# Round 0 of an RWKV6 and MLP kernel: taken whole, in place of its first 128 steps going ahead

## The chip, the cores and the metric

The kernel runs on one core of a Trainium2 chip. Its engines are TensorE (PE, with its weight loads shown apart as PEld), VectorE (DVE), ScalarE (ACT), GpSimd (POOL) and SyncE (SP, which here only starts transfers). The metric is device time in microseconds (us), lower is better. A time is the median of some runs; a profile is one execution of its own.

## The reference

An attention block without softmax (a decaying state, step by step) over 4 batches, 8 heads, 768 steps and 48 dimensions of a head, and then a layer norm and an MLP with a residual, all in float32.

```python
for t in range(S):
    kt, vt, rt, wt = (k[:, :, t], v[:, :, t], r[:, :, t], w[:, :, t])
    cur = np.einsum('bhd,bhe->bhde', u[None] * kt, vt)
    y[:, :, t] = np.einsum('bhd,bhde->bhe', rt, state + cur)
    state = wt[:, :, :, None] * state + np.einsum('bhd,bhe->bhde', kt, vt)
...
xn = (x - mu) / np.sqrt(var + 1e-06) * g_ln
ch = np.maximum(xn @ w_ch1, 0.0) @ w_ch2
return (x + ch).astype(np.float32)
```

Here `x` is `y` with the 8 heads side by side (384 columns), `w_ch1` is 384 x 1536 and `w_ch2` 1536 x 384.

## The kernel before

**Tiles and rounds.** The work is cut into 8 rounds: a batch and a half of its steps (384 steps, three tiles of 128) for all 8 heads. A round has two units of four heads, each with two pairs of heads. In a chunk of 64 steps the recurrence is written as products: squares of steps against steps, built up over six levels (`quads` on PE, `grow` on DVE, `keep` on DVE), and a state passed between chunks (`states`).

**A round in order.** Natural tiles of w, k and r are loaded (`load`, tile `nat`), turned by PE through an identity (`turn`, tiles `w_ps`, `k_ps`, `r_ps`) and copied from the accumulation banks by ACT (or DVE in round 0). `totals` multiplies the decays up level by level (`tot`, `decay`; DVE or POOL). At every level PE multiplies squares (tile `a`), DVE scales k and r by the decay (`grow`) and copies the squares that this level gives into `A`, by a mask (`keep`). ACT copies the last level. k is turned back (`turn_k`, `kn_ps`), then PE makes the chunks' states, DVE scans them (`s`, `last`), ACT exchanges halves (`rx`, `sx`), PE makes the outputs, and DVE adds the step's own term (`own`, `own_term`, tiles `rk`, `vo`) and writes `x`. `normalize` and `turn_x` give `xf`. The MLP has a first product (`h_ps` to `h`, 12 blocks) and a second one (`o`).

**The MLP's weights** come in as 24 blocks of 384 KB (`convert`, tile `raw`, four buffers). Each is put into another form by three ACT and two DVE instructions: 12 blocks of w_ch1 (`w`, `held`) and 12 of w_ch2 (`ffn`, `rest`). From round 1 on the first product runs in three cheaper products of split operands, for which w_ch1 is split by `halve` (`wh`, `wl`).

**What sets the order.** The order of all instructions is written by a planner (`Plan.order`) as the program is built. It goes through the operations with costs and priorities written beside them, gives each to an engine when its operands, its buffer and its engine are free by these costs, takes the one with the lowest priority number first, and so fixes the order of each engine's queue. An operation with `port=True` also keeps DVE and POOL from running port operations side by side in the plan. The queues run in order on the chip; SP's queue holds all loads but some of round 0's, which ACT starts. Where the plan leaves PE without work for over 0.4 us before its 90th us, it puts in products of nothing (`idle`). There are two pairs of accumulation banks for the tile `a` and four banks for the others.

**Round 0 in two parts.** `parts_of_round` gives round 0 two parts, the first 128 steps of all heads and the other 256, and every other round one. `front`, `normalize`, `turn_x` and `first_product` are called once for each part, and the first part has a round's lead in priority (`urgent`). Its loads (`load_first`) take all 8 heads at once, one for each of w, k and r, into tiles held for them from the start. The shifts and joins of the first six weight blocks have priority -6. The masks of the levels (`build_mask`) are built by POOL with priority `lev - 40` and `port=False`.

Of the kernel before, what the change touches and what calls it, by code (L numbers as in the profile page):

```python
# [9 lines left out]
F32 = mybir.dt.float32  # L10
# [6 lines left out]
ALU = mybir.AluOpType  # L17
# [243 lines left out]
def kernel(  # L261
# [57 lines left out]
    def tile_(tag, name, shape, dtype=F32):  # L319
        if name in tiles:  # L320
            return tiles[name]
        if tag == "a":
            tiles[name] = a_homes[plan.place[name]]
            return tiles[name]
        if tag == "nat" and name.startswith("nat_"):
            tiles[name] = nat_homes[plan.place[name]]
            return tiles[name]
        if tag == "b":
            t = banks.tile([P, 512], dtype, tag=f"b{plan.place[name]}", name=name)
            tiles[name] = t[:, 0 : shape[1]]  # L330
            return tiles[name]
        t = homes.tile(shape, dtype, tag=f"{tag}{plan.place[name]}", name=name)
        tiles[name] = t
        return t
# [11 lines left out]
    plan.hold("vo", "nat_r_0")  # L346
    tile_("vo", "nat_r_0", [P, NH * ROW])
    for name in ("nat_r_1", "nat_k_1", "nat_w_1", "nat_k_0", "nat_w_0"):
        plan.hold("nat", name)
        tile_("nat", name, None)  # L350
# [27 lines left out]
    for nm in "wkr":  # L378
        POOL.memset(tiles[f"nat_{nm}_0"][:, 0 : HP - D], 0.0)
    for nm in "wk":  # L380
        POOL.memset(tiles[f"nat_{nm}_0"][:, NH * ROW :], 0.0)
# [33 lines left out]

    SRC = {"w": w, "k": k, "r": r}
    NA = U * NP

    def parts_of_round(rnd):
        return [(rnd, 0, TT)] if rnd else [(0, 0, 1), (0, 1, TT - 1)]

    def urgent(part, stage):
        rnd, c0, nc = part
        return at(rnd - (nc == 1), stage)

    def cost(part, fixed, whole):
        return fixed + (whole - fixed) * part[2] / TT

    def of(part, t, per):

        _, c0, nc = part
        return t.rearrange("p (a x) -> p a x", a=NA)[:, :, c0 * per : (c0 + nc) * per]

    def keys_of(nm, part, us=both_units):
        rnd, c0, _ = part
        return [(f"{nm}{rnd}", NP * uu + pr, c0) for uu in us for pr in pairs]

    def groups_of(part):  # L440

        n = min(NP if part[0] == 0 else 1, NA) if part[2] > 1 else NA
        return [(a, n) for a in range(0, NA, n)]

    GAP = HP - D

    def natural(nm, part, a):

        rnd, c0, _ = part
        if rnd == 0:  # L450
            return f"nat_{nm}_{c0}", a
        return f"nat_{nm}{U * rnd + a // NP}", a % NP

    def row_of(part):

        return part[2] * D, (GAP if part[2] == 1 else 0)

    def load_first(nm, part, eng, pri):
        _, c0, nc = part
        b, f = rounds[0]  # L460
        name = natural(nm, part, 0)[0]
        queue = SP if eng == "SP" else ACT
        row, margin = row_of(part)

        def go():
            queue.dma_start(
                out=tiles[name][:, margin : margin + H * row].rearrange("p (h x) -> p h x", h=H),
                in_=SRC[nm][b, :, ds(f * RN + c0 * P, nc * P)]
                .rearrange("h (p c) d -> p h (c d)", p=P),
            )  # L470

        plan.add(eng, 0.5, go, w=[name], r=[], pri=pri, lat=2.0, size=0.8 + 0.3 * (nc > 1))

    def load(nm, q):
        b, f, g = units[q]
        name = f"nat_{nm}{q}"

        def go():
            to = tile_("nat", name, None)
            if q // U < ROWS:  # L480
                SP.dma_start(
                    out=to[:, 0 : NH * ROW].rearrange("p (h x) -> p h x", h=NH),
                    in_=SRC[nm][b, ts(g, NH), ds(f * RN, RN)]
                    .rearrange("h (p c) d -> p h (c d)", p=P),
                )
                return
            for c in range(TT):
                SP.dma_start(
# [4 lines left out]
        cost_, size = (0.5, 0.8) if q // U < ROWS else (1.65, 1.2)  # L493
        plan.add(
            "SP", cost_, go, w=[name], new=[("nat", name)], pri=at(q // U, "wrk".index(nm)), lat=2.0,
            size=size,
        )
# [4 lines left out]
    def turn(nm, part, a0, na, stage):  # L502
        rnd, c0, nc = part
        name, ps = f"{nm}{rnd}", f"{nm}_ps{rnd}_{c0}_{a0}"
        rows = rnd < ROWS
        row, margin = row_of(part)

        def go():
            t = tile_("b", ps, [P, na * nc * P])
            for a in range(na):  # L510
                key, pr = natural(nm, part, a0 + a)
                for c in range(nc):
                    to = ts(a * nc + c, P)
                    if not rows:
                        both = by_tile(tiles[key])[:, c, ts(pr, 2)].rearrange("p j d -> p (j d)")
                        PE.transpose(t[0:PD, to], both[:, 0:PD], ident)
                        continue


                    at_ = 2 * pr * row + c * D + margin  # L520
                    second, first = ds(at_ + row - HP, PD), ds(at_, HP)
                    PE.transpose(t[0:PD, to], tiles[key][:, second], ident)
                    PE.transpose(t[0:HP, to], tiles[key][:, first], ident)

        def keep(e="ACT"):
            to = of(part, tile_(nm, name, [P, U, W])[0:PD].rearrange("p u t -> p (u t)"), P)
            to, ps_ = to[:, a0 : a0 + na], tiles[ps][0:PD].rearrange("p (a x) -> p a x", a=na)
            if rows and nc > 1:
                to = to.rearrange("p a (s c) -> p a s c", c=nc)
                ps_ = ps_.rearrange("p a (c s) -> p a s c", c=nc)  # L530
            (DVE.tensor_copy if e == "DVE" else ACT.copy)(out=to, in_=ps_)

        n = na * nc
        keys = [(name, a0 + a, c0) for a in range(na)]
        new = [(nm, name)] if a0 == c0 == 0 else []
        plan.add(
            "PE", 0.11 * n * (1 + rows), go, count=2 * n * (1 + rows),
            r=[natural(nm, part, a0)[0]] + keys, w=[ps], new=[("b", ps)] + new,
            pri=urgent(part, stage), lat=0.17,
        )  # L540
        copy = 0.1 + 0.12 * n
        plan.add(
            ("ACT", "DVE") if rnd == 0 else "ACT", (copy, copy + 0.05) if rnd == 0 else copy, keep,
            r=[ps], w=keys, pri=urgent(part, stage) + EVICT / 2,
        )

    def totals(part):
        rnd, c0, nc = part
        tot, dec = f"tot{rnd}", f"decay{rnd}"
        costs = list(zip((1.0, 0.55, 0.4, 0.3, 0.25, 0.2), (1.5, 0.9, 0.58, 0.42, 0.34, 0.25)))  # L550
        for lev in range(NLEV):
            def go(e, lev=lev):
                if lev == 0:
                    tile_("tot", tot, [P, U * W])
                    tile_("decay", dec, [P, U * NM])
                pair = level_total(part, lev).rearrange("p a (q two) -> p a q two", two=2)
                BY[e].tensor_tensor(
                    out=level_total(part, lev + 1), in0=pair[..., 0], in1=pair[..., 1], op=ALU.mult
                )
            plan.add(  # L560
                EITHER, [cost(part, 0.17, x) for x in costs[lev]], go,
                r=keys_of("w", part) if lev == 0 else [(tot, lev, c0)],
                w=[(tot, lev + 1, c0)] if lev < NLEV - 1 else [(dec, c0)],
                new=[("tot", tot), ("decay", dec)] if lev == c0 == 0 else [],
                pri=urgent(part, 6 + lev),
            )

    def level_total(part, lev):
        rnd = part[0]
        if lev == 0:  # L570
            t = tiles[f"w{rnd}"].rearrange("p u t -> p (u t)")[0:PD]
        elif lev == NLEV:
            t = tiles[f"decay{rnd}"][0:PD]
        else:
            n = U * W >> lev
            t = tiles[f"tot{rnd}"][0:PD, U * W - 2 * n : U * W - n]
        return of(part, t, P >> lev)

    def own(part, us):
        rnd, c0, nc = part  # L580
        heads, h0 = NH * len(us), NH * us[0]
        kk, kr = (natural(nm, part, NP * us[0])[0] for nm in "kr")
        rk, o, row = f"rk{rnd}_{c0}_{us[0]}", f"own{rnd}", f"own_row{rnd}"
        rows = rnd < ROWS
        by_row = rows and nc > 1
        row_, margin = row_of(part)
        margin += (rnd == 0) * h0 * row_

        def parts():

            t = tile_("rk", rk, [P, NH * ROW])[:, 0 : nc * heads * D]
            if rows:
                views = [
                    t_.rearrange("p (h c d) -> p c h d", h=heads, c=nc) for t_ in (
                        tiles[kk][:, margin : margin + heads * row_],
                        tiles[kr][:, margin : margin + heads * row_], t,
                    )
# [4 lines left out]
            return views + [u_bc[:, None, ds(h0, heads)].broadcast_to([P, nc, heads, D])]  # L602
# [9 lines left out]
        def third():  # L612
            if by_row:
                t = tile_("own_row", row, [P, TT, H])[:, 0:nc]
            else:
                t = tile_("own", o, [P, TT, H])[:, c0 : c0 + nc]
# [1061 lines left out]
```

## Time and profile before

| | us |
|---|---|
| median of 3 runs | 537.83 |
| lowest and highest | 537.31, 539.05 |
| the profiled execution, whole | 537.31 |
| its span in the profile | 535.4 |

How to read the profile: one execution is recorded instruction by instruction, in us from the span's start. Busy time is the time in which an engine has at least one instruction under way; consecutive instructions overlap a little, so a row's start-to-start distance is shorter than its duration. All operations are recorded by one helper (line 49), so groups are told apart by tile names: `k<-k,tot` reads `k` and `tot` and writes `k`. `x6` is the number of instructions in a merged row; a float32 product takes two. PE's groups by busy time:

| group | instructions | busy us |
|---|---|---|
| second product of rounds 0 to 4, `o<-ffn,h` | 360 | 124.7 |
| squares, states and outputs, `a`, weight loads 63.1 | 4608 (squares) | 69.4 |
| first product of round 0, 128x128 | 72 | 9.4 |
| first product of round 0, 128x256 | 72 | 18.3 |
| `idle` | 34 | 13.1 |

The last row adds its three shapes (9.0, 3.0 and 1.1). POOL's ten mask selections, eight mask copies and two `mask_and` lie between 1.85 and 11.1 us.

### The profile page before, as it was taken

Reading aid. Unit: us, or ns where it says so; the run is one execution under the profiler, and the core shown is the slowest. Engines: PE = TensorE matmul, PEld = TensorE weight load, DVE = VectorE, ACT = ScalarE, POOL = GpSimd, SP = SyncE. Lnnn points to the kernel's source line nnn. Section 1 sums busy time; section 2 is a strip of 40 time slices with the busy share of each in tenths; the row PEclk is TensorE's granted clock in tenths of the full one; section 3 lists DMA queues with packets and bytes.
Section 4 is the critical chain, followed back from the end, with each engine's and each line's share of the span. In section 5 each row is a group of like instructions: output and inputs, shape, how many; then the busy total and the mean of one; then the engine's idle time right before and its main releaser. Section 6 shows DMA issues by size and latency. Waiting matters only on the chain.

```text
span 535.4 us, 20629 instructions
## 1 busy us (share of the span) xinstructions
PE 521.3 (97%) x8994; PEld 434.4 (81%) x8994; DVE 403.2 (75%) x845; ACT 269.0 (50%) x602; POOL 73.0 (14%) x106
## 2 busy tenths in 40 slices
PE   8999899999999999999999999999999999999995
PEld 6778788776989676889766998669867999999994
DVE  6898969797999988999765787546555856656554
ACT  3798868962395532663630885046721434332321
POOL 6212201531203041112110000002200000000000
PEclk9999989999999999999999999999999999999999
DMA  9874864378525646576111415014101322213101
GB/s 222 248 209 142 192 175 105 72 185 237 158 49 105 157 85 131 113 148 146 61 30 37 112 39 139 2 40 115 46 15 60 104 60 88 89 45 108 56 0 45
DMA packets 122362, 55.84 MB, mean 104 GB/s; under 512 B 93984, under 2 KB 119200, under 8 KB 122272
## 3 DMA queue, kind: packets, MB, share of 16 engines
q1 hardware_dynamic: 119152, 53.54, 39.3%
q10 hardware_dynamic: 3120, 0.98, 1.0%
q8 instruction: 71, 1.16, 0.9%
q14 instruction: 19, 0.16, 0.1%
HBM read 45.05 MB, written 7.10 MB: 97 GB/s over the span
## 4 chain that ended last, share of the span: by engine, by line
PE 85%; DVE 7%; DMA 2%; issue 1%; POOL 1%; SPq 1%; ACT 1%; DVEq 0%; POOLq 0%; ACTq 0%
PE a L49 24%; PE o L49 21%; PE h_ps L49 18%; PE hd_ps L49 7%; PE w_ps L49 3%; PE k_ps L49 2%; PE r_ps L49 2%; PE o_2P L49 2%; PE kn_ps L49 2%; DVE x L49 2%; PE xT_ps L49 2%; PE idle L49 1%; DVE k L49 1%; PE o_2D L49 1%; DVE r L49 1%
## 5 line engine op out<-in xcount | busy, mean ns | idle before, releaser
L49 PE MATMUL o<-ffn,h 128*128 128x384 f32 x360 | 124.7, 491 | 0.0
L49 PEld LDWEIGHTS o<-ffn,h 128*128 128x128 f32 x360 | 65.4, 190 | 37.6
L49 PEld LDWEIGHTS a<-r,k 48*60 48x60 f32 (+5 forms) x4608 | 63.1, 126 | 19.6 <-issue 8.5
L49 ACT COPY h<-hd_ps 128x384 f32<-128x384 f32 x84 | 39.9, 479 | 71.6 <-PE hd_ps L49 69.8
L49 DVE SCALAR_TENSOR_TENSOR h<-h_ps,h 128x384 f32<-128x384 f32 x84 | 46.5, 555 | 34.7 <-PE h_ps L49 34.2
L49 PE MATMUL a<-r,k 48*60 48x32 f32 (+5 forms) x4608 | 69.4, 212 | 2.0 <-DVE r L49 1.3
L49 DVE TENSOR_TENSOR k<-k,tot 112x768 f32<-112x768 f32 (+1 forms) x50 | 41.4, 828 | 29.0 <-PE a L49 18.6
L49 PE MATMUL h_ps<-xhl,wl 128*128 128x384 f32 x252 | 60.8, 349 | 0.3
L49 PE MATMUL h_ps<-xhl,wh 128*128 128x384 f32 x252 | 57.9, 338 | 0.0
L49 PE MATMUL hd_ps<-xd,d 128*128 128x384 f32 x252 | 55.4, 347 | 0.0
L49 PEld LDWEIGHTS h_ps<-xhl,wl 128*128 128x128 f32 x252 | 43.7, 188 | 3.5 <-ACT h L49 1.1
L49 PEld LDWEIGHTS h_ps<-xhl,wh 128*128 128x128 f32 x252 | 45.3, 188 | 0.0
L49 PEld LDWEIGHTS hd_ps<-xd,d 128*128 128x128 f32 x252 | 43.9, 188 | 1.1
L49 DVE COPY_PREDICATED A<-mask,a 128x768 f32<-128x768 int8 (+2 forms) x36 | 39.3, 1092 | 0.9 <-PE a L49 0.9
L49 DVE TENSOR_TENSOR r<-r,tot 112x768 f32<-112x768 f32 (+1 forms) x50 | 39.6, 791 | 0.0
L49 ACT ACTIVATE hH<-h 128x384 fp32r<-128x384 f32 x36 | 18.8, 526 | 41.0 <-DVE h L49 41.0
L49 ACT ACTIVATE h<-h 128x384 f32<-128x384 f32 x48 | 25.1, 526 | 20.3 <-DVE h L49 20.1
L49 POOL TENSOR_TENSOR vo<-v,own 128x576 f32<-128x576 f32 (+1 forms) x12 | 13.5, 1121 | 141.3 <-DVE x L49 107.3
L49 ACT COPY w<-w_ps 112x384 f32<-112x384 f32 (+1 forms) x31 | 14.3, 489 | 34.3 <-PE w_ps L49 34.0
L49 DVE SCALAR_TENSOR_TENSOR hL<-h,hH 128x384 fp32r<-128x384 f32 x36 | 20.0, 555 | 14.3 <-ACT hH L49 14.0
L49 ACT COPY A<-a 32x384 f32<-32x384 f32 (+2 forms) x36 | 15.6, 433 | 27.8 <-PE a L49 27.5
L49 PE MATMUL h_ps<-xf,w 128*128 128x128 f32 (+1 forms) x144 | 27.7, 343 | 0.1
(120 smaller groups left out, 1020.3 us busy)
## 6 DMA issues: line engine op xcount, KB each, us to landing
d<-w1d SPq DMA_DIRECT2D x84, 192.0 KB, 2.7
raw<-in_moe_w_ch_dram SPq DMA_DIRECT2D x24, 384.0 KB, 4.3
v<-in_v_dram SPq DMA_DIRECT2D x48, 96.0 KB, 2.8
out_dram<-x SPq DMA_DIRECT2D x24, 192.0 KB, 1.9
nat<-in_w_dram SPq DMA_DIRECT2D x36, 96.0 KB, 3.5
nat<-in_k_dram SPq DMA_DIRECT2D x36, 96.0 KB, 3.2
nat<-in_r_dram SPq DMA_DIRECT2D x36, 96.0 KB, 3.0
w1d<-w1diff SPq DMA_DIRECT2D x12, 192.0 KB, 2.7
```

The lines of the kernel that those rows point to most:

```text
L49: ins = self.tc.keep_in_program_order(f(*args, **kw))
```

## The change

Round 0 becomes one part like the other rounds. `front`, `turn`, `totals`, `own`, `quads`, `grow`, `keep`, `keep_last`, `exchange_r`, `turn_k`, `load_v`, `own_term`, `states`, `outputs`, `normalize` and `turn_x` lose the part and work on a round or on a unit; `first_product` goes back into `mlp`. Round 0's six loads are one for each of w, k, r and each unit, of 384 steps and four heads, from SP for one unit and ACT for the other. Only the two r tiles have homes held from the start, and five fills on POOL (128x192) take the place of three of 128x16 and two of 128x192. The masks' priority is `lev` and no longer `lev - 40`, still with `port=False`; the shifts and joins of the first six weight blocks have the priority of the others; `g` is loaded with priority 20 and no longer -10. Tiles in the four banks have the shape asked for and no longer a whole bank, and the squares lie in the first 384 columns of a bank. The planner and its costs for the other rounds stay.

```diff
-    plan.hold("vo", "nat_r_0")
-    tile_("vo", "nat_r_0", [P, NH * ROW])
-    for name in ("nat_r_1", "nat_k_1", "nat_w_1", "nat_k_0", "nat_w_0"):
-        plan.hold("nat", name)
-        tile_("nat", name, None)
+    for q in both_units:
+        plan.hold("vo", f"nat_r{q}")
+        tile_("vo", f"nat_r{q}", [P, NH * ROW])
...
-    for nm in "wkr":
-        POOL.memset(tiles[f"nat_{nm}_0"][:, 0 : HP - D], 0.0)
-    for nm in "wk":
-        POOL.memset(tiles[f"nat_{nm}_0"][:, NH * ROW :], 0.0)
+    for t in nat_homes:
+        POOL.memset(t[:, NH * ROW :], 0.0)
...
-    def parts_of_round(rnd):
-        return [(rnd, 0, TT)] if rnd else [(0, 0, 1), (0, 1, TT - 1)]
-
-    def urgent(part, stage):
-        rnd, c0, nc = part
-        return at(rnd - (nc == 1), stage)
...
-        first = -6 if i < FC // 2 else pri
...
-        plan.add("DVE", 0.32, shift, w=[key], pri=first, port=True)
-        plan.add("DVE", 0.56, join, r=[rest_], w=[key], pri=first, port=True)
+        plan.add("DVE", 0.32, shift, w=[key], pri=pri, port=True)
+        plan.add("DVE", 0.56, join, r=[rest_], w=[key], pri=pri, port=True)
...
-    def first_product(part):
-        rnd, c0, nc = part
-        steps = slice(c0 * P, (c0 + nc) * P)
-        for f in range(FC):
...
+                def go(f=f, ps=ps, g=g, cols=cols):
+                    t = tile_("b", ps, [P, RN])
+                    for kc in range(KC):
+                        PE.matmul(
+                            t, tiles[f"w1_{g}"][:, kc, cols], tiles[f"xf{rnd}_{kc}"],
+                            start=kc == 0, stop=kc == KC - 1,
+                        )
...
-    def front(part):
-        rnd, c0, nc = part
+    def front(rnd):
...
             for i, nm in enumerate("wkr"):
-                load_first(nm, part, ("SP", "ACT")[(i + c0) % 2], at(c0 - 1, i))
-        if rnd == c0 == 0:
+                for q, eng in zip(qs, ("SP", "ACT")):
+                    load(nm, q, eng, i)
+        if rnd == 0:
...
-                plan.add(
-                    "POOL", 1.7, lambda lev=lev: build_mask(lev), r=["wide"], w=[("mask", lev)],
-                    pri=lev - 40, port=False,
-                )
+                plan.add("POOL", 1.7, lambda lev=lev: build_mask(lev), r=["wide"], port=False, w=[("mask", lev)], pri=lev)
...
-        w=["g"], pri=-10, lat=2.0, size=0.2,
+        w=["g"], pri=20, lat=2.0, size=0.2,
...
-    for part in parts_of_round(0):
-        front(part)
-        norm(part)
-        if part[1] == 0:
-            for i in range(len(parts)):
-                convert(i)
-        first_product(part)
-    mlp(0)
+    front(0)
+    for i in range(len(parts)):
+        convert(i)
+    back(0)
```

## Prediction

> **What bounds the kernel now.** I read the page's busy shares and chain first, then busy time by stretches, the chain in order of time, and the timeline where the change acts.
>
> ```profile
> PE 521.3 (97%) x8994; PEld 434.4 (81%) x8994; DVE 403.2 (75%) x845; ACT 269.0 (50%) x602; POOL 73.0 (14%) x106
> ...
> PEclk9999989999999999999999999999999999999999
> ...
> PE 85%; DVE 7%; DMA 2%; issue 1%; POOL 1%; SPq 1%; ACT 1%; DVEq 0%; POOLq 0%; ACTq 0%
> ```
>
> TensorE (PE) sets the time. What can change it is only PE's own work, and the time in which PE has none: its gaps and its filler products (tile `idle`). The stretches say where those are:
>
> ```profile
> 15.00:65.00 50.00, 48.42 (x1178) 40.00 (x1171) 45.46 (x126) 44.26 (x110) 10.43 (x14) 1.00 0.71 191
> 61.30:69.30 8.00, 5.13 (x114) 4.12 (x115) 7.86 (x11) 4.85 (x11) 1.43 (x1) 0.97 0.80 189
> 69.30:77.60 8.30, 8.30 (x129) 7.00 (x128) 3.80 (x6) 6.24 (x15) 0.00 (x0) 0.83 0.82 212
> 77.60:96.10 18.50, 18.50 (x458) 16.23 (x456) 17.02 (x26) 16.58 (x39) 4.27 (x3) 1.00 0.37 93
> 96.10:535.40 439.30, 431.13 (x7084) 359.19 (x7083) 322.43 (x663) 194.88 (x429) 48.77 (x52) 1.00 0.35 88
> ```
>
> Columns: stretch, length, busy PE, weight loads, VectorE (DVE), ScalarE (ACT), GpSimd (POOL), granted clock, DMA share, GB/s. From 77.6 us PE is saturated, with 8.2 us open in the last 439.3. So the change is decided before about 96 us, where round 0's second product starts. In 15 to 65 DVE (91%) and ACT (88.5%) are both nearly full. The chain, then the timeline:
>
> ```profile
> 28.96 2.58 PE idle L49 x8
> ...
> 62.63 4.93 DMA nat<-in_k_dram
> ...
> 76.45 1.30 PE h_ps L49 x6
> ...
> 93.44 1.15 PE kn_ps L49 x12
> ...
> 96.11 2.13 PE o L49 x6
> ```
>
> ```profile
> 35.33 0.42 DVE L49 TENSOR_TENSOR r<-r,tot 112x256 f32<-112x256 f32 x1
> 35.67 0.42 DVE L49 TENSOR_TENSOR k<-k,tot 112x256 f32<-112x256 f32 x1
> 61.49 0.95 DVE L49 TENSOR_TENSOR k<-k,w 112x768 f32<-112x768 f32 x1
> 62.36 0.95 DVE L49 TENSOR_TENSOR r<-r,w 112x768 f32<-112x768 f32 x1
> ```
>
> ```profile
> 60.57 0.59 SPq L49 DMA_DIRECT2D raw<-in_moe_w_ch_dram  x1
> 61.34 1.25 SPq L49 DMA_DIRECT2D vx<-v  x2
> 62.63 1.80 SPq L49 DMA_DIRECT2D nat<-in_k_dram  x3
> ```
>
> Until about 33 us PE is filled up with `idle`: it waits for the first 128 steps to pass through attention. At 62.6 it waits for a load of k that SP could issue only after a weight load (`raw`), whose buffer ACT had to free.
>
> **PE's lost time before.** I count PE's own work by rows and subtract it. 72 turning instructions a round at 0.13 (x6 in 0.80): 9.4. The six levels' squares (x96): 1.58, 1.56, 1.45, 1.37, 1.21, 0.95: 8.1. Turning k back 1.15, states 1.3, outputs 2.9, xT 1.1. Round 0 without its first product: 24.0. First product: 12 x 0.72 (36 instructions in 4.29) for 128 steps and 12 x 1.30 for 256. At 61.3 us PE has done 24.0 + 8.6 + round 1's turning 9.4 and level 0 1.6 = 43.6, so 17.7 us are lost. At 77.6 it has 55.0 (four more blocks 5.2, levels 1 and 2 3.0, 24 turnings of round 2 3.2), so 22.6 are lost: 4.9 between, 1.4 of them in the 0.83 clock of 8.3 us.
>
> **The change, part by part.**
>
> *The masks.* Their instructions stand in the same place on POOL in both programs, ahead of all tensor work; only the fills before them differ (five of 128x192 at 0.26 for three of 0.11 and two of 0.26: +0.45 us). Before, the last mask lands at 11.1 us; after, the first level that needs one copies from about 21. Cost nothing, covered by 9 us. So the masks move nothing; what moves is round 0.
>
> *First product whole.* 36 products of 128x384 (1.94 for x6, as the rows of `o`) for 36 of 128 and 36 of 256: 12 x (0.72 + 1.30 - 1.94) = 1.0 us of PE saved.
>
> *When it can start (T).* Four parts:
> (a) Six loads of 288 KB go first (SP w, k, r; ACT the same for the other unit), then u, four weight blocks and six v, each issue past the eighth waiting for the landing of an older one. DMA moved 214, 210, 242, 320 GB/s in the four slices of 2 to 10 us, 1.97 MB, against 1.77 MB needed: the last r lands near 9. PE starts turning at about 4.4 as now, 12 groups x 0.80 to 14.0, last eviction 0.48, half of level 0 0.79: 15.3.
> (b) Then DVE. Scaling k or r of one unit is 112x384; start to start it takes 0.34 at 256 and 0.87 at 768, so 0.47: 24 make 11.3. Squares of 768: 0.87 + 1.82 + 3 x 0.90 = 5.4. A reduction, a shift and waits for PE (1.5 us in the present second part, 31.5 to 46.7) 3.0. Ends at 35.0. From below: the two parts take 12.4 and 15.2 for one and two thirds, a line through them gives 18.0, so 33.3.
> (c) States, outputs, norm. Round 1's level 0 holds one of the two pairs of banks, so both units' states and outputs go one after the other through the other. DVE: own terms and conversion 2.8, scan 12 x 0.19 = 2.25, 0.75, scan 2.25, 1.5, x 0.8, 2.25 conversions, x 0.8, statistics 1.8: 50.2; root and normalize 2 to 2.4; on ACT a conversion and a half (2.7) lie before the three xf (0.47 each): T = 56. From below by the line through the parts (last scaling to first product 10.8 and 14.6, so 18.4): 52. From above by ACT, which holds 42.4 us of work from 14.3 to the last xf (15 conversions of 1.755, 14 evictions of 0.48, 14 copies 7.4, 2.0): at its 88.5% share 62. I take 58, between hand sum and ACT's bound, since DVE and ACT hand each other every step.
> By T PE has done 24.0 + 9.4 + 1.6 + 0.8 = 35.8, so T - 35.8 = 22.2 is lost: as much as before in all. End = T + (535.4 - 77.6) + 55.0 - 1.0 - 35.8 = T + 476.0 = 534.0.
>
> A clock row first: after PE's gap near 65 to 67.7 it is granted 0.83 for 8.3 us. [...]
>
> *The wait for round 2's loads.* Moved in SP's queue: after the change seven `raw` loads stand in a row ahead of round 2's second k and both r, each waiting for ACT to convert an earlier block; behind them wait k's turning on PE, and all behind that. Round 2's w and first k go earlier (good for one half of it). The cause of the 62.6 us wait stays. Bounds: 0 (with T = 56 and a conversion each 1.57 us on ACT, 0.45 + 1.12 start to start in the timeline, and one eviction a block, the seventh block is issued at about 66.5; the k behind it lands 4.9 us later as now, at 72; PE comes to it after four blocks, two levels and eight small steps, at 73) to the 4.9 us that the same order costs now. The nearest row is this wait, with ACT as full as then: I take 4.9.
>
> *Later rounds.* The same instructions; squares lie in banks by 384 instead of 4 x 32 columns, same element counts. They are hidden by PE's saturation; the 8.2 us open after 96.1 bound a gain, of which 5.2 are the tail. Cost 0, from -2 to +3.
>
> **Sum:** 534.0 + 4.9 = 538.9 against the profiled span of 535.4: +3.5. The profiled run took 537.31, the median of the three is 537.83; so 541.3.
>
> **Rivals.**
> 1. *Faster.* Round 1's and 2's tiles arrive in time, as (a)'s early loads speak for, and T is the hand sum 56: 532.0, run 534.4; with T = 52, 530.4. For it: DVE does 24 scalings at 0.47 in place of 48 at 0.34, 5 us less. Against: the tightness at 73.
> 2. *No change.* T = 58 and the wait half as long, or T = 61 and none: 536.5 to 537, run 538 to 539. The lost time is only moved from many fillers to one. For it: 22.2 against 22.6 lost.
> 3. *Much slower: ACT becomes the bound.* From T to the second product ACT holds xf, nine conversions, twelve first-product evictions, halving of w1: 42 us by durations for 37.8 of PE. Place: PE's four banks wait for ACT's evictions. It decides once T's delay pushes conversions behind the evictions; price 4 to 5 on top, with T = 62: 538.0 + 4.9 + 4 = 546.9, run 549. Against: start to start ACT's conversions take 1.57, not 1.755.
> 4. *The change does not do what it says*: so for the masks; it adds no time of its own.
>
> **How the numbers follow.** Forecast (541.3, own range 539 to 545) 0.44; much slower 0.18; no change 0.13; faster 0.25. Range 533.5 to 548: at the low end the hand sum less what later rounds may give, at the high end ACT's bound. A measurement can tell 0.3%, 1.6 us. Faster 0.25, within 0.13, slower 0.62.
>
> **What would show it.** First product starts at 56 to 60 us (before 33.4 and 61.3); `idle` and gaps before it make 20 us or more; second product (`o`) starts 99 to 101 instead of 96.1; PE waits for k or r of round 2 between 65 and 80, clock under 0.9 there. Wrong if `o` starts by 95 without such a wait (rival 1), or if POOL's masks hold up a copy.

## The result and the profile after

| | before | after |
|---|---|---|
| median (20 runs each) | 537.98 us | 541.87 us |
| lowest, highest | 535.59, 540.66 | 538.23, 544.49 |
| profiled execution, whole | 537.31 | 539.55 |
| its span | 535.4 | 537.8 |
| mean granted clock of it | 0.995 | 0.997 |

The changed kernel takes 1.006 times as long (95% interval 1.0038 to 1.0082): 3.9 us between the medians, 2.4 between the two spans. The forecast was 541.3 (own range 539 to 545). An execution over 1.5% above the fastest of its kernel is left out of the ratios and counts below; three kernels have one each.

The chain of waits of the changed kernel (start, duration, work) up to the second product:

```profile
41.69 2.36 PE idle L49 x8
...
50.55 3.81 DMA raw<-in_moe_w_ch_dram
...
57.67 1.52 PE idle L49 x6
59.19 7.74 PE h_ps L49 x24
...
96.98 1.94 PE o L49 x6
```

One first product, at 59.2, where there were two, and the second product 0.9 us later than before (96.11). The wait for k at 62.6 is gone. SP's and PE's timelines of the changed kernel show why:

```profile
58.68 10.70 SPq L49 DMA_DIRECT2D raw<-in_moe_w_ch_dram  x7
70.97 1.48 SPq L49 DMA_DIRECT2D nat<-in_k_dram  x3
72.49 3.25 SPq L49 DMA_DIRECT2D nat<-in_r_dram  x6
```

```profile
75.13 0.87 PE L49 MATMUL k_ps<-ident,nat 128*112 128x128 f32 x6
```

The seven `raw` loads do stand ahead of k and r, and k does go out as late as 71. But a bracket with a wait is missing in PE's row: PE comes to it at 75.1 out of other work and finds it there, 0.5 us after the last of its three pieces landed (74.65). Nor do the `raw` loads set the time of this k: the last of them has left by 69.4, and SP then waits for PE itself, which still has to read a w out of the tile that this k is to fill:

```profile
SPq L49 <- PE w_ps L49: 1.8, 1, 1.8
```

The extra time lies further back. PE's busy time in stretches, before and then after (stretch; its length; PE, PEld, DVE, ACT and POOL busy with counts; clock; DMA share; GB/s):

```profile
140.00:150.00 10.00, 9.40 (x235) 8.34 (x233) 9.93 (x13) 5.16 (x12) 1.42 (x1) 1.00 0.29 79
150.00:165.00 15.00, 15.00 (x484) 13.70 (x484) 14.17 (x41) 11.92 (x28) 2.26 (x4) 1.00 0.36 69
...
250.00:260.00 10.00, 10.00 (x230) 8.92 (x229) 9.27 (x12) 4.43 (x10) 2.88 (x2) 1.00 0.40 114
260.00:270.00 10.00, 10.00 (x187) 7.38 (x186) 6.86 (x13) 8.03 (x19) 1.47 (x1) 1.00 0.12 40
```

```profile
140.00:150.00 10.00, 10.00 (x187) 9.32 (x179) 9.17 (x32) 8.04 (x19) 3.60 (x7) 1.00 0.40 106
150.00:165.00 15.00, 13.77 (x375) 11.96 (x370) 12.46 (x22) 7.02 (x17) 3.73 (x3) 1.00 0.71 139
...
250.00:260.00 10.00, 7.80 (x130) 5.52 (x128) 6.02 (x8) 5.11 (x12) 4.29 (x3) 1.00 0.14 35
260.00:270.00 10.00, 9.54 (x228) 8.38 (x226) 7.64 (x28) 6.11 (x14) 0.23 (x1) 1.00 0.06 14
```

Over 100 to 500 us PE stands still for 4.55 us after and 2.14 before; that difference, 2.4, is as large as that of the spans. The two new places are 150 to 165 (a load of r for round 4, issued by SP at 157.9 behind a load and a copy of v) and 250 to 257, whose chain in the changed kernel is

```profile
248.79 3.37 DMA nat<-in_r_dram
...
252.32 1.42 POOL rk L49
...
253.81 1.42 POOL rk L49
...
255.92 0.96 DVE k L49
...
256.93 0.79 PE kn_ps L49 x6
```

DVE's and PE's timelines have the two waits in brackets:

```profile
255.25 0.75 DVE L49 TENSOR_REDUCE own<-rk 128x12 f32<-128x576 f32 x1 [2.74 <-POOL rk L49]
256.93 0.79 PE L49 MATMUL kn_ps<-ident,k 112*128 112x112 f32 x6 [2.20 <-DVE k L49]
```

DVE's queue has the reduction `own` of unit 14 (wanted at 300 us) ahead of the scaling of k that PE wants now; `own` waits 2.7 us for GpSimd's `rk`, and PE 2.2 for the scaling.

### The profile page after: what moved, and what is told of

It is laid out like the page before. It is cut to its first block, busy times and chain, and to the rows that moved or that the text cites. A ratio compares the mean times of both kernels' runs of the same rounds, so it can differ in the third digit from the quotient of the medians.

```text
span 537.8 us, 20417 instructions
## 1 busy us (share of the span) xinstructions
PE 522.9 (97%) x8938; PEld 428.6 (80%) x8938; DVE 400.1 (74%) x819; ACT 266.6 (50%) x579; POOL 74.9 (14%) x98
## 4 chain that ended last, share of the span: by engine, by line
PE 87%; DVE 5%; DMA 2%; SPq 2%; issue 1%; ACT 1%; POOL 1%; DVEq 0%; POOLq 0%; ACTq 0%
PE a L49 23%; PE o L49 22%; PE h_ps L49 19%; PE hd_ps L49 7%; PE w_ps L49 3%; PE k_ps L49 2%; PE r_ps L49 2%; SPq L49 2%; PE o_2P L49 2%; PE kn_ps L49 2%; PE xT_ps L49 2%; DVE x L49 1%; DMA nat<-in_r_dram 1%; PE o_2D L49 1%; DVE s L49 1%
## 5 line engine op out<-in xcount | busy, mean ns | idle before, releaser
L49 PEld LDWEIGHTS o<-ffn,h 128*128 128x128 f32 x360 | 65.7, 190 | 37.8
L49 PEld LDWEIGHTS a<-r,k 48*56 48x56 f32 (+5 forms) x4608 | 63.0, 126 | 15.7 <-issue 9.2
L49 PE MATMUL a<-r,k 48*56 48x32 f32 (+5 forms) x4608 | 68.6, 212 | 1.5 <-issue 1.2
L49 PE MATMUL h_ps<-xhl,wl 128*128 128x384 f32 x252 | 61.4, 351 | 0.8 <-DVE h L49 0.5
L49 ACT ACTIVATE h<-h 128x384 f32<-128x384 f32 x48 | 25.1, 524 | 29.6 <-DVE h L49 29.4
L49 DVE COPY_PREDICATED A<-mask,a 128x768 f32<-128x768 int8 x32 | 38.7, 1210 | 1.1 <-PE a L49 1.1
L49 POOL TENSOR_TENSOR rk<-nat,nat 128x576 f32<-128x576 f32 x11 | 15.6, 1421 | 119.7 <-DMA d<-w1d 45.9
L49 ACT COPY A<-a 32x384 f32<-32x384 f32 x32 | 15.0, 468 | 31.6 <-PE a L49 30.5
L49 POOL TENSOR_TENSOR vo<-v,own 128x576 f32<-128x576 f32 x9 | 11.3, 1255 | 113.1 <-DVE x L49 87.5
L49 PE MATMUL a<-w2d,hD 128*128 128x384 f32 x72 | 25.5, 354 | 0.8 <-DVE hD L49 0.7
```

The source lines that it names most:

```text
L49: ins = self.tc.keep_in_program_order(f(*args, **kw))
```

## The experiments

Twelve kernels, each timed against the kernel before on the same chip. The kernel before had medians of 538.6 to 539.1 there.

### The changed kernel again, and the small edits apart from the split

> The changed kernel once more, to see how far its executions differ and whether the clock goes with it. Theory A (round 0 whole puts 24 us of waiting before the first product and about 2 us of late tiles behind the second): first product at 59 (58.5 to 59.5), second at 96.8 (96 to 97.5), the rest 441 (440 to 442), profiled span 536.5 to 539; the median stays 1.004 to 1.009 of the kernel before. Rival C (a lower granted clock is what makes the median longer): executions with a mean clock of 0.990 or less take 542 or more, those at 0.996 or more 540 or less, in both kernels alike; if the kernel before has as many low ones, the clock explains nothing of the difference.

Measured: 1.0065 (1.0038 to 1.0092). The profiled execution has its first product at 60.0, the second at 97.8, span 539.1. Over this and the first comparison the time of 31 executions goes with the clock: those at 0.999 to 1.000 take 538.2 to 539.4 us, those at 0.986 to 0.989 take 543.9 to 546.3. The kernel before shows a like line, at the upper end more often: 49 of its 98 executions in the four series below are at 0.996 or more, and 10 of these 31. So the clock has a part in the median, but a small one. The mean clocks are 0.9951 and 0.9938, and 0.001 of clock goes with 0.4 to 0.5 us in either kernel, so it explains some 0.6 us of the 3.3 between the mean times (538.9 and 542.2). At a clock of 0.998 or more the kernels still take 536.8 (15 executions) and 539.1 (4). What makes the clock fall was still open.

```diff
-        first = -6 if i < FC // 2 else pri
+        first = pri
...
-                    pri=lev - 40, port=False,
+                    pri=lev, port=False,
...
-        w=["g"], pri=-10, lat=2.0, size=0.2,
+        w=["g"], pri=20, lat=2.0, size=0.2,
```

> The kernel before, round 0 still in two parts, with the change's small edits alone: the first six weight blocks' shifts and joins no longer lead on DVE, the gain g is loaded at a low priority, the masks have the priority of their level. Theory A (the split is all): time within 0.3% of the kernel before (536.4 to 539.6), second product at 95.5 to 97. Rival B (the small edits carry the difference): 1.004 to 1.008 of the kernel before (540 to 542), with the first product's first part later than 33.4 because DVE comes late to its weight blocks.

Measured: 1.0096 (1.006 to 1.0132), span 543.5. Theory A's zero is wrong, and so is rival B's picture: the second product starts at 90.1, 6 us sooner than before, and PE then stands still for 11 us between 100 and 500. A milestone reached sooner says nothing where the order behind it is another. (The change's new shapes of the bank tiles are in neither this kernel nor any other run by themselves.)

```diff
+        first = -6 if i < FC // 2 else pri
-        plan.add("DVE", 0.32, shift, w=[key], pri=pri, port=True)
-        plan.add("DVE", 0.56, join, r=[rest_], w=[key], pri=pri, port=True)
+        plan.add("DVE", 0.32, shift, w=[key], pri=first, port=True)
+        plan.add("DVE", 0.56, join, r=[rest_], w=[key], pri=first, port=True)
...
-        w=["g"], pri=20, lat=2.0, size=0.2,
+        w=["g"], pri=-10, lat=2.0, size=0.2,
```

> The changed kernel, round 0 whole, with the small edits taken back: six weight blocks' shifts and joins lead on DVE, and g is loaded early. Theory A: within 0.3% of the changed kernel (540 to 543 where that takes 541.5), first product at 58 to 61. Rival B (the lead matters): back to within 0.2% of the kernel before (537 to 539). A third way: 12 shifts and joins of 0.88 a pair put 5.3 us ahead of the scalings on DVE, so that the first product starts at 62 to 64 and the time is 544 to 547.

Measured: 1.0156 (1.0122 to 1.019). (The masks stay as the change has them.) The first product starts at 59.6 and the second at 96.6, as in the changed kernel; of the 7.5 us between the two profiles some 5 lie in 150 to 300 us, where PE stands still for 6.0 us (4.1 in the changed kernel) and the mean clock is 0.97 for 100 us. With round 0 split the small edits cost 1%, and with round 0 whole taking them back costs 0.9%. So they have no price of one sign. I read it so: each writes the planner's whole order anew, and the time is what late waits that order happens to hold; these two runs fit that, they don't prove it. From here on single instructions are moved in the finished order, all else kept.

### What the wait at 62.6 us was

```diff
-            SP.dma_start(
+            (POOL if i >= 4 else SP).dma_start(
                 out=tile_("raw", raw_, [P, WC, 2], I32).rearrange("p n two -> p (n two)"),
```

> The kernel before with one thing moved: from the fifth weight block on, the loads into raw are issued by GpSimd's queue, so that round 2's k and r no longer stand behind them in SP's queue. This prices the wait at 62.6 us. If it is worth its 4.9 us of PE (as the prediction had it): the wait is gone, second product at 91 to 93, time 532.5 to 534.5. If PE's lost time up to the second product is set by DVE and ACT and the wait only stands where they would have made one anyway: second product at 95 to 96.5 and time within 0.3% of the kernel before (536.4 to 539.6).

Measured: 1.0055 (1.0024 to 1.0086), second product at 98.98. SP's timeline in this kernel:

```profile
55.16 5.18 SPq L49 DMA_DIRECT2D v<-in_v_dram  x6
60.53 3.50 SPq L49 DMA_DIRECT2D vx<-v  x4
64.08 2.05 SPq L49 DMA_DIRECT2D nat<-in_k_dram  x3
```

No `raw` is left in front of k, and k goes out at 64.1 where it went at 62.6. This execution is 1.5 us late before that (the second part of the first product starts at 62.8, not 61.3), so k goes out as far behind that start as before, 1.2 against 1.3 us. PE then waits 2.2 us for k in two pieces (2.3 before), and the clock falls behind that as it did before (a mean of 0.83 in 70 to 80 us; before, 0.94 in 60 to 70 and 0.89 in 70 to 80). So the weight load wasn't what held k; in the kernel before, SP's waits for ACT from 45 us up to k make 0.7 us in all. Ahead of k stand v (SP's waits before it are put down to PE's `a` and DVE's `vo`, which read the old v) and `vx`, which copies v once it has landed. Neither outcome that I had written down came; the chain also has two late loads of r (4.4 and 5.4 us), and what of those comes from the loads that GpSimd now starts isn't parted.

```diff
+        for old, new in ((371, 347),):
+            out.insert(new, out.pop(old))
         return [fn for _, fn in out]
```

(371 is the load of k in the finished order, 347 the first copy of v.)

> The kernel before with round 2's first load of k (issued at 62.63, landed 67.56, PE waiting for it) moved in SP's queue ahead of two copies of v and one load of raw: it can go once GpSimd has read round 1's k in the same buffer, at about 59. If the wait costs what the prediction put on it (4.9, of which this frees 3 to 4): k lands at 63 to 65, second product at 92.5 to 93.5, time 533.5 to 535 where the kernel before takes 538 (0.991 to 0.994). If what comes behind it (the second k, issued at 68.7, DVE, ACT, or the copies of v now later) holds PE up instead: second product at 95 to 97, ratio 0.997 to 1.003.

SP's timeline of this kernel, and a wait that its PE timeline then shows:

```profile
59.78 1.48 SPq L49 DMA_DIRECT2D nat<-in_k_dram  x3
61.31 1.26 SPq L49 DMA_DIRECT2D vx<-v  x2
...
64.60 2.55 SPq L49 DMA_DIRECT2D nat<-in_w_dram  x3
```

```profile
68.54 0.56 PE L49 MATMUL w_ps<-ident,nat 128*112 128x128 f32 x2 [0.80 <-DMA nat<-in_w_dram]
```

Measured: 0.9976 (0.9955 to 0.9997), span 533.7 against 535.4. k goes out 2.85 us sooner and the second product starts at 93.35, 2.76 sooner; part of it is given back at 208 us, where PE loses 1.1 (below). In these two profiles the wait was worth 2.8 us at its place and 1.7 at the end, not 4.9.

Not all of the 2.8 is waiting. From 57 us to the second product PE stands still for 2.96 us in the kernel before and 1.43 here, which makes 1.5; the other 1.2 is PE's busy time, 36.15 against 34.92 for the same products. PE's wait of before and the clock behind it show why:

```profile
67.69 0.87 PE L49 MATMUL k_ps<-ident,nat 128*112 128x128 f32 x3 [2.30 <-DMA nat<-in_k_dram]
```

```profile
68.00:69.00 1.00, 0.93 (x7) 0.77 (x8) 1.00 (x2) 0.07 (x1) 0.00 (x0) 0.88 1.03 214
69.00:70.00 1.00, 1.00 (x5) 0.91 (x4) 1.00 (x1) 1.00 (x3) 0.00 (x0) 0.50 0.86 246
...
71.00:72.00 1.00, 1.00 (x4) 0.66 (x3) 0.00 (x0) 0.00 (x0) 0.00 (x0) 0.50 1.16 271
72.00:73.00 1.00, 1.00 (x23) 0.82 (x23) 0.00 (x0) 0.82 (x3) 0.00 (x0) 0.92 0.51 101
```

Behind a wait of 2.3 us the clock is at half from 68.8 to 72.2. Here it stays at 1.00, and 11 of 12 executions have a mean clock of 0.996 or more (16 of 29 of the kernel before on this chip).

### The late waits of the changed kernel

```diff
+        for old, new in ((1121, 1142),):
+            out.insert(new, out.pop(old))
         return [fn for _, fn in out]
```

(1121 is the reduction `own` of unit 14; 1142 a step of `totals`.)

> The changed kernel with one DVE instruction moved back in its queue: the reduction `own` of the last unit but one (round 7, not needed before 300 us), which stands at 255 us ahead of the scalings that PE waits for and itself waits 2.7 us for GpSimd's `rk`. Theory D (the time lies in late waits behind the second product that the new order made, 2.2 us of them here): PE busy 9.5 or more of 10 us in 250 to 260 (7.8 now), span 1.5 to 2.2 shorter than the changed kernel's (535.5 to 537.5), ratio to the kernel before 1.002 to 1.004. Theory A in its first form (the delay of the first product is what costs; later waits only take up slack): the wait turns up again within the next 50 us, span and ratio as the changed kernel (1.0045 to 1.0085).

Measured: 1.0054 (1.0021 to 1.0088), not told apart from 1.0065. PE's wait at 256 shrinks from 2.2 to 0.2 us, and one of 2.0 stands at 265 in place of 0.5: where I put it, `own` lies in the chain of totals and scans that `h` waits for. Then the profiled execution shows what the clock does (stretches of 1 us, columns as above):

```profile
265.00:266.00 1.00, 0.28 (x2) 0.00 (x0) 1.00 (x8) 0.87 (x3) 0.00 (x0) 1.00 0.00 0
266.00:267.00 1.00, 0.00 (x0) 0.00 (x0) 1.00 (x6) 0.87 (x3) 0.00 (x0) 1.00 0.00 0
267.00:268.00 1.00, 0.70 (x4) 0.70 (x5) 1.00 (x2) 0.95 (x3) 0.00 (x0) 1.00 0.00 0
268.00:269.00 1.00, 1.00 (x20) 0.75 (x22) 1.00 (x3) 0.30 (x1) 0.00 (x0) 0.78 0.00 0
269.00:270.00 1.00, 1.00 (x49) 1.00 (x46) 0.44 (x1) 0.52 (x1) 0.00 (x0) 0.50 0.00 0
...
274.00:275.00 1.00, 1.00 (x5) 0.98 (x4) 0.23 (x1) 0.43 (x1) 0.00 (x0) 0.50 0.15 32
275.00:276.00 1.00, 1.00 (x44) 0.58 (x44) 0.00 (x0) 0.52 (x3) 0.00 (x0) 0.81 0.00 0
```

A wait of 2.0 us, and 1.3 us later the clock is at half for 6.8 us (0.22 + 6 x 0.50 + 0.19 = 3.4 us lost). The changed kernel's own 2.2 us wait at 255 left the clock at 1.00 in its profile, and so did one of 2.5 in the profile of its repeat. In these three profiles a wait of 2.0 to 2.5 us cost itself alone or itself and 3.4 us. (The same profile has a shorter fall, from 29.6 to 33.0, behind a wait of 1.8 us in the squares of round 0.)

```diff
+        for old, new in ((1121, 1142), (748, 731)):
+            out.insert(new, out.pop(old))
         return [fn for _, fn in out]
```

(748 is the load of r at 157.9, 731 the load of v ahead of it.)

> As the one before, and the second load of r for round 4 issued by SP ahead of a load and a copy of v instead of behind them (issued at about 153.5 instead of 157.9; PE waits for it until 161.9 in the changed kernel). Theory D: another 1 us, PE busy 14.6 or more of 15 us in 150 to 165 (13.8 now), ratio to the kernel before 0.999 to 1.002, that is, the whole difference is gone with round 0 still whole. Theory A in its first form: ratio 1.0045 to 1.0085. If v is late instead: a new wait of PE between 160 and 180 and no gain over the one before.

Measured: 1.0014 (0.9988 to 1.0039). Its stretches:

```profile
150.00:165.00 15.00, 14.87 (x406) 13.67 (x398) 13.33 (x26) 8.38 (x20) 3.06 (x3) 1.00 0.66 134
...
250.00:260.00 10.00, 9.18 (x264) 7.39 (x254) 9.01 (x10) 4.03 (x9) 3.12 (x3) 1.00 0.39 81
```

The first wait is gone, the second cut from 2.2 to 0.8. This profile too holds a fall of the clock: 0.50 from 28.7 to 35.5, behind 1.5 us of waiting in the squares of round 0, and the first product starts at 63.0.

### The clock

```diff
-    for fn in plan.order(busy, ("b", 0.24, idle), 90.0):
+    for fn in plan.order(busy, ("b", 0.24, idle), 5.0):
```

> The changed kernel without its `idle` products behind 5 us (they fill PE's waits with matmuls nobody reads, at 20 to 24, 42 to 44 and 57.7 to 59.2 us). By the row of the kernel before (after a gap of 5 us PE ran 8.3 us at 0.83, 1.4 us lost): the first product starts at 58.5 to 60 as now, the clock is under 0.9 for 4 to 9 us behind one or two of the gaps, time 1.5 to 4 longer (ratio 1.009 to 1.014). If the clock stays at 1.00 behind gaps of 2 us, or if PE is not what is waited for there: time as the changed kernel (1.0045 to 1.0085).

Measured: 1.0166 (1.0125 to 1.0208), above both. Stretches of it:

```profile
50.00:55.00 5.00, 2.46 (x85) 2.30 (x80) 3.79 (x12) 4.45 (x10) 0.83 (x3) 0.50 0.89 238
55.00:60.00 5.00, 2.94 (x10) 2.21 (x11) 4.72 (x14) 3.85 (x9) 0.00 (x0) 0.50 0.93 257
60.00:65.00 5.00, 5.00 (x11) 2.64 (x11) 3.85 (x9) 3.63 (x9) 0.00 (x0) 0.65 0.75 237
```

(PE's gap of 5 us that the text above names is one of 2.3 in the row shown earlier.) The clock is at half from 49.8 to 63.5, so the first product runs its first 4 us at half speed (its longest instruction takes 1.01 us, the median 0.49); its start (59.5) hardly moves, as PE has nothing to do for 4.6 of the 10 us before 60. Two more falls, of 6.8 us each, start at 19.1 and 223.9, and all 6 executions have mean clocks of 0.963 to 0.980. But the planner counts the `idle` products, and without them it writes another order on every queue. So the 1% between this kernel and the changed one is `idle` and a new order together, and no run parts them. The next two put four more `idle` products in two places:

```diff
+            if op.i in (74, 783):
+                home = min(self.homes[idle[0]])[1]
+                fn = lambda fn=fn, home=home: (idle[2](4, home), fn())
```

> The changed kernel with both moves of the last series and four `idle` products (1.14 us) in each of two places where PE waits about 2 us unfilled: ahead of the second half of level 3's squares at 27 us, and ahead of the first product of row 8 at 265 us. Theory E (the spread of the changed kernel's executions, and the part of the median that the spans do not explain, is the clock falling to 0.50 for some 6 us behind such a wait in some executions): most executions at a mean clock of 0.996 or more, highest to lowest within 4 us (6.4 without the fill), median 537 to 538.5, ratio to the kernel before 0.996 to 1.000. Rival (the clock falls by chance, whatever PE does, or the fill holds PE up by as much as it saves): clocks and spread as without it, ratio 0.999 to 1.004.

Both moves and the fill: 0.9994 (0.9969 to 1.0018), median 538.39. Eleven of 12 executions at 0.996 or more (6 of 12 with the moves alone, 10 of 31 in the changed kernel). The spread stayed at 5.4 us, above the 4 expected, by one execution at 543.0. The profile shows that other waits are left: its clock is at half from 41.6 to 45.0, behind one of 1.2 us.

> The changed kernel, its order untouched, with four `idle` products (1.14 us) ahead of the second half of level 3's squares at 27 us and four ahead of turning k back at 255 us, where PE waits 2.2 us. It parts the clock's share from the waits' share: the waits stay, only their length without any matmul falls under 1.5 us. Theory E (the clock falls behind those waits in some executions): most executions at 0.996 or more, median 1 to 2.5 us below the changed kernel's, ratio to the kernel before 1.002 to 1.0045, the rest being the waits themselves. Rival (the clock has no part, the moves of the series before did it all): 1.0045 to 1.0085 with clocks of 0.986 to 1.000 as without the fill.

The fill alone (before operations 74 and 1321): 1.0041 (1.001 to 1.0071), 9 of 11 executions at 0.996 or more. The clocks changed plainly; the interval of the time overlaps that of the changed kernel.

### The same cure on the kernel before

Round 5's second `rk` stood at 207 us ahead of scalings, the same fault as `own`.

```diff
+        for old, new in ((371, 347), (379, 348), (1023, 1030)):
+            out.insert(new, out.pop(old))
         return [fn for _, fn in out]
```

> The kernel before with three moves, no instruction added: round 2's first k and the w behind it ahead of the copies of v (SP), and at 207 us the second `rk` of round 5 behind the scalings of level 4 instead of ahead of them (DVE waited 2.3 us for GpSimd there, PE 1.1). If late waits are what the time is made of: PE does not wait for w at 68.5, second product at 92 to 93, PE busy 4.6 or more of 5 us in 205 to 210, time 0.992 to 0.996 of the kernel before. If the copies of v come too late by it: PE waits for vx between 66 and 80, second product no earlier than 93.3, ratio 0.996 to 1.000.

> The same without the move of w: second product at 93.3 as with k alone, the 1.1 us at 208 regained: 0.9945 to 0.9975 of the kernel before. If the wait of DVE for `rk` is only taken up by the next wait (r's scaling, the reduction): as with k alone, 0.9955 to 0.9997.

Measured: 0.9977 (0.9955 to 0.9998) and 0.9969 (0.9948 to 0.9989). The wait at 208 is gone in both, but in both profiles PE now waits for the second k of round 2 (landed at 74.9 and 75.5; 2.1 and 1.1 us) and the second product comes at 95.4 and 95.9. The last kernel has the order of the one with k alone in all that comes before 200 us, and yet its second product is 2.5 us later: 1.9 of it were lost before 63.3, where the second part of the first product starts (61.4 there). So a place in one profile moves by some 2 us from execution to execution, and the 2.8 us that moving k gave at its place are those of one pair of profiles.

These two and the one with k alone are faster than both kernels; none of the three is told apart from the others. Most of what they gain on the kernel before goes with the clock: 11, 12 and 11 of their 12 executions are at 0.996 or more. At 0.998 or more the one with k alone takes 536.6 us (10 executions), these two 537.4 (8) and 537.6 (7), and the kernel before 536.8 (15).

## Why the prediction came out right, and where its steps failed

**Right: the start of the first product.** T was put at 58; it is 59.0 to 59.2 in the profile, and 58.7 to 63.0 in the six profiles with this order up to there (two have four `idle` more), so in part outside the 56 to 60 given. The hand sum of 56 was short in one step: the last scaling ends at 38.1 and not at 35.0, and half of that is DVE waiting 3.0 us for PE's squares where 1.5 were put. From there to T it takes 21 us, as summed. That 58 made up for two of the three us was a choice between sum and bound, not worked out, and so in part luck. Behind T PE has no wait until the second product, and so any delay of T is passed on whole: T and the second product are 59.19 and 96.98, 60.01 and 97.81, 61.53 and 99.34, 63.00 and 100.80 in four of these profiles, 37.8 apart in each. That was the base of "End = T + 476.0". Behind it the four differ: span less T is 478.6, 479.1, 481.1 and 476.6, as the later waits and the clock do.

**Right: the masks.** The planner with priority `lev` and with `lev - 40` writes one and the same order on all five engines, in both kernels. They move nothing.

**Failed: the wait for round 2's loads, 4.9 us.** I read 62.6 as "behind a weight load whose buffer ACT had to free" and said that the cause stays. It was not the weight load (with `raw` on another queue the wait is as long), and the wait doesn't come after the change: no wait of PE stands between 60 and 97, the clock stays at 1.00 there, and the second product starts at 97.0 and not at 99 to 101. The step that failed is to carry a wait over because loads of the same kind stand ahead of it. The own lower bound, 0, held. Its reasoning (seventh block issued near 66.5, k landed at 72, PE there at 73) left PE 1 us to spare, and it has 0.5; but k goes out when PE frees its tile, which the reasoning hadn't. The price was wrong as well: between the two marks PE stands still for 2.9 us, of which 2.3 are this wait, and the fall of the clock behind it adds some 1.2. Freeing it gave 2.8 us at the spot in one profile.

**Failed in size: later rounds, 0.** They cost 2.4 us of waits, inside the -2 to +3 that I kept. "The same instructions" was the wrong ground: the order is new in all rounds, and an order is where waits come from. The sum was 58 + 476.0 + 4.9 = 538.9; it is 59.0 + 476.0 + 2.8 = 537.8, 0.4 of the 2.8 not assigned. The term that failed and the one that was left at nothing stood in for each other but for 2.1 us; T was 1.0 later. That the sum came within 1.1 us of the span is luck.

**Failed: the clock left out.** The sum has no term of its own for a fall of the clock. That is right for the gap before T, where the program has `idle` and the clock is 1.00 from 45 to 60, and wrong for the others: waits of 1 to 2.5 us inside the squares at 27 and at 255 or 265 have no fill, and behind some of them the clock falls (to 0.50 for 3.4 and 6.8 us in the first kernel with `own` moved). The spans differ by 2.4 us and the medians by 3.9. Lower clocks explain some 0.6 us between the two kernels, as above; the rest is that a profile is one execution. The prediction added 2.4 for what lies between span and median (it is 4.1 here) and hit the median through a term that was too large. The row of 0.83 over 8.3 us is a mean over a stretch that was cut too wide: read us by us, that stretch of the kernel before is 0.50 from 68.8 to 72.2 and 1.00 behind (the lines above).

**Rivals.** "Faster" and "much slower by ACT" didn't occur. "No change" did not either, but its ground (the lost time only moves from many fillers to one) is what the runs bear out: with two instructions moved, round 0 whole is at 1.0014 (0.9988 to 1.0039), and with two gaps filled besides at 0.9994. So most of the cost was in the order that came with round 0 whole; that the step itself costs nothing isn't shown. Whether either form of round 0 is better at its best stays open: 0.9994 (0.9969 to 1.0018) against 0.9969 (0.9948 to 0.9989), each with two moves, the first alone with the fills. At a clock of 0.998 or more these take 538.4 us (9 executions) and 537.6 (7).

## What to carry to other kernels

Where a planner writes the order, a changed priority or split has two prices: that of the step, and that of a new order with other late waits. Look for these in the finished order: an instruction that isn't due soon, standing in a queue ahead of one that PE needs, and waiting for another engine or a load (here 2.7 us for GpSimd's `rk`); moving it alone gives a fair test. Before a wait is blamed on the load in front of it, list all that stands ahead in the queue and what each waits for. Before two profiles are compared, look at the clock in each, us by us: one fall of 6.8 us (3.4 us lost) is as large as the effects sought here (2.4 between the spans, 3.9 between the medians).

## What the runs showed of the hardware

Behind a wait of PE of 2.0 us without any matmul the clock fell to 0.50 in one execution (for 6.8 us, 3.4 us of work lost), and behind one of 2.3 us in another (for 3.4 us), while waits of 2.2 and 2.5 us left it at 1.00 in two more. In stretches of broken work it also fell behind waits of 1.8, 1.5 and 1.2 us. The falls read last 3.4 us (from 68.8, 29.6 and 41.6 in three profiles) or 6.8 us (from 28.7 and 268.6), and 13.6 us where PE had little to do (from 49.8): once, twice and four times the shortest. At 0.50 six instructions of 128x256 took 2.77 us in the kernel before, at 1.00 1.56. What decides whether the clock falls behind a wait, no run here shows.
